# The low parts of the first phase's weights: ScalarE writes the rounded weights negated, and a DMA from GpSimd's queue adds the weights from DRAM

## The chip, the core and the metric

The kernel runs on one core of a Trainium2 chip. The metric is the time of one execution on the device, in microseconds (us). Three runs of the kernel before took 1390.13, 1390.4 and 1390.64 us; the median is 1390.4 us.

## The reference

Three layers run one after the other, all in float32.

```python
# 1. linear attention, 4 batches x 8 heads, 768 steps, head size 48
for t in range(768):
    state = alpha[t][:, None] * state + outer(k[t], v[t])
    y[t]  = q[t] @ state
x = y as (3072 tokens, 384)
# 2. four experts, 384 -> 1024 -> 384, all of them for every token
p = probs / (probs.sum(-1) + 1e-9)
x = sum over e of  p[:, e] * (relu(x @ w1[e]) @ w2[e])
# 3. one layer, 384 -> 2048 -> 384
h = x @ w_in;  out = (h * clip(h + 3, 0, 6) / 6) @ w_out
```

## The kernel before

Every large matmul is done in three passes of a faster number format. A float32 matrix A is split into a rounded part `hi` and the remainder `lo` = A - hi, and A @ B becomes hi@hi + lo@hi + hi@lo. For a weight slice `round_w` makes both parts: ScalarE copies the loaded slice into the rounding format (L770), VectorE subtracts (L772). The tiles are called w0h and w0l for a slice of w1, w1h and w1l for one of w2; the loaded slice is `rw`, or a room in a tile `early_h` or `early_l`. x is split in the same way into xh and xl (L789, L790), and the hidden layer into hh (ScalarE, from the matmul's result ph) and hl (VectorE, from ph and hh; L822, L825).

The experts' hidden units are cut into 16 slices of 256. The first phase goes with the first S0 = 7 slices over all tokens, while the attention of later tokens is still being computed; phases 1 and 2 take the other slices and the last layer. A step is half a slice (128 hidden units) for one block of tokens: `mm1` makes ph, then hh and hl; `mm2` of the step before adds into the accumulators po. The first block of 512 tokens is done in two halves of 256 tokens, which are one attention unit each, so the first pass over the 7 slices is 14 steps. In these steps the weights of the slices are still being split for the first time.

Attention runs in units of 256 tokens. One unit's work is a list of named pieces: products of q, k and alpha on VectorE, transposes and small matmuls on TensorE (pkt, pqt, pa, pk, pu, py), copies of their results on ScalarE (kt, qt, kc, qc, ktok, ys), and per unit one trip of the result to DRAM (x_d) and back (rx). `Attention.group` and `Attention.rest` put some pieces of the next unit behind each step.

TensorE, VectorE, ScalarE and SP carry out their instructions in the order in which the program writes them down (`manual_schedule`); a planner sets GpSimd's order. The list `todo` holds pairs of a step and a function: `next_w` splits one loaded slice at its step and, where that frees a room, issues the load of a later slice on SP's queue. Loads of slices 1 to 3 are issued before the steps begin. GpSimd clears tiles and cuts masks for the attention at the start, and decodes part of the last layer's weights much later; it issues no DMA.

Of the kernel before, what the change touches and what calls it, by code (L numbers as in the profile page):

```python
# [14 lines left out]
AF = mybir.ActivationFunctionType  # L15
# [3 lines left out]
P = 128  # L19
# [536 lines left out]
def tile_gla__then__moe__then__moe2(  # L556
# [29 lines left out]
    nc = tc.nc  # L586
# [4 lines left out]
    KT = DM // P  # L591
    NB = 512
    NBLK = N // NB
    SL = 2 * P
    S0 = 7
# [4 lines left out]
    mul, add, sub = ALU.mult, ALU.add, ALU.subtract  # L600
# [42 lines left out]
    w_out32 = dram.tile([F2, DM], F32, name="w_out32")  # L643
# [89 lines left out]
    wts, raws = {}, {}  # L733
# [6 lines left out]
    def rw(nm):  # L740
        nonlocal nraw
        if early:
            return early.pop(0)
        nraw += 1
        pool = rawq if late and nraw % 3 == 0 else rawp
        return pool.tile([P, 3 * SL], F32, tag="rw", name=nm)

    def load_w(y, i):
        e, c = slices[i]
        raw = rw(f"rw{y}_{i}")  # L750
        if y == 0:
            src = w_in32 if e is None else w1[e]
            nc.sync.dma_start(
                raw.rearrange("p (j f) -> p j f", j=KT), src[:, c : c + SL].rearrange("(j p) f -> p j f", p=P)
            )
        else:
            src = w_out32 if e is None else w2[e]
            nc.sync.dma_start(
                raw.rearrange("p (j m) -> p j m", j=2), src[c : c + SL, :].rearrange("(j p) m -> p j m", p=P)
            )  # L760
        raws[(y, i)] = raw

    def split_w(y, i):
        round_w(y, i)()

    def round_w(y, i):
        raw = raws.pop((y, i))
        pool = wpb if S0 <= i < S0 + SB or S1 <= i < S1 + SB else wpa
        hi, lo = (pool.tile([P, 3 * SL], F32R, tag=f"w{y}{z}", name=f"w{y}{z}_{i}") for z in "hl")
        nc.scalar.copy(hi, raw)  # L770
        wts[(y, i)] = [t.rearrange("p (j f) -> p j f", j=KT if y == 0 else 2) for t in (hi, lo)]
        return lambda: nc.vector.tensor_tensor(lo, raw, hi.bitcast(F32), op=sub)  # L772


# [159 lines left out]
            nc.sync.dma_start(out[r0 : r0 + P, :], o)  # L934


    ctx.enter_context(tc.manual_schedule(engines={mybir.EngineType.DVE, mybir.EngineType.Activation, mybir.EngineType.PE, mybir.EngineType.SP}))
    at_ctx = ExitStack()
    at = Attention(at_ctx, tc, q, k, v, alpha, x_d, psa, "psa", lambda n: load_x(0, n), lambda n: split_x(0, n))
    NU = at.NU  # L940
# [1 line left out]
    at.load_vd(0)  # L942
    at.load(0, "v")
    load_w(0, 0)
    nc.sync.dma_start(pr, probs.rearrange("(p i) e -> p i e", p=P))
    at.load_vt(0)
    load_w(1, 0)
    for z in "hl":
        e_ = xp.tile([P, KT * NB], F32, tag=f"x{z}", name=f"early_{z}")
# [3 lines left out]
    def again(x):  # L953

        early.append(rooms[x])
# [4 lines left out]
    def sw(y, i):  # L960
        split_w(y, i)
# [11 lines left out]
    busy(6)  # L973
    at.load(1, "qka")
    load_w(0, 1)
    load_w(1, 1)
    load_w(0, 2)
# [6 lines left out]
    busy(5)  # L984
    u("C3 y1 M2 K")
    lows = [round_w(0, 0), round_w(1, 0)]
    busy(5)
    u("y2 y3 y4 y5 U")
# [7 lines left out]
    at.load(1, "v")  # L996
    at.load_vd(1)
    low = round_w(0, 1)
    u("p2 r1 u0 u1 cp kq kk tp", 1)
    low()  # L1000
# [16 lines left out]
    todo = []  # L1017
# [28 lines left out]
    def next_w(y, i):  # L1046
        sw(y, i)
        if (y, i) in room_of and queue:
            room_of[queue[0]] = room_of[(y, i)]
            again(room_of[(y, i)])  # L1050
            load_w(*queue.pop(0))

    for y, i in order[order.index((1, 1)) :]:
        todo.append((2 * i - 2 + y, lambda y=y, i=i: next_w(y, i)))
    pend, rest = [], []
    period, at_step, begun = 0, 0, g
    last_b = (0, 0)
# [1 line left out]
    for vi, vv in enumerate(visits):  # L1059
# [16 lines left out]
        for f in range(len(vv["steps"])):  # L1076
# [29 lines left out]
            i, z = v2["steps"][done[1]]  # L1106
# [55 lines left out]
```

## Time and profile before

| | |
|---|---|
| median of three runs | 1390.4 us |
| the profiled execution | 1391.08 us, its span 1389.1 us |
| TensorE (PE) busy | 1360.7 us, 98% |
| VectorE (DVE) busy | 843.7 us, 61%, and 90% or more in many of the first slices |
| ScalarE (ACT) busy | 453.0 us, 33% |
| GpSimd (POOL) busy | 83.0 us, 6% |
| mean granted clock of TensorE | 0.993 of full speed |

Times in the rows are us from the start of the span. A row of the timeline has the start, the length, the engine, the line, the operation, what is written and read, and in square brackets how long the engine idled before and what ended that. A row of the stretches has the stretch, its length, then busy time and number of instructions of PE, PEld (weight loads), DVE, ACT and POOL, then TensorE's granted clock, the mean busy share of the 16 DMA engines, and GB/s. A row of the waits has the sum, the number of waits and the longest. SPq is SP's queue of DMA issues.

### The profile page before, as it was taken

How to read it: one execution, taken by the hardware profiler on the slowest of the kernel's cores; microseconds unless marked ns; L12 is line 12 of the kernel's file. 1: busy time of each engine (PE TensorE's matmuls, PEld its weight loads, DVE VectorE, ACT ScalarE, POOL GpSimd, SP SyncE). 2: the span in 40 equal slices, each digit the busy share in tenths (PEclk: the TensorE clock that was granted, in tenths of full speed). 3: DMA queues.
4: the chain of work that ended last, by engine and by line, in shares of the span. 5: the costliest groups of instructions: out<-in, count | busy, mean ns of one | idle time of the engine just before them, and what ended most of it. 6: DMA issues, size and time to landing. Idle time of an engine off the chain costs nothing.

```text
span 1389.1 us, 26360 instructions
## 1 busy us (share of the span) xinstructions
PE 1360.7 (98%) x11006; PEld 1137.7 (82%) x11006; DVE 843.7 (61%) x1524; ACT 453.0 (33%) x775; POOL 83.0 (6%) x125
## 2 busy tenths in 40 slices
PE   8788999999999999999999999999999999999998
PEld 7788887888878888888888888888888888888898
DVE  8998977767685268657566666645534343434332
ACT  3554444443434133111111111113333333333333
POOL 2000000000000001211111111100000000000000
PEclk9989999999999999999999999999999999999999
DMA  6654544344532256514242422324202020202010
GB/s 196 189 153 127 155 133 134 103 113 133 146 111 89 66 186 213 158 54 151 64 141 65 125 92 89 101 65 133 91 1 46 1 46 0 46 1 46 1 23 24
DMA packets 156551, 132.36 MB, mean 95 GB/s; under 512 B 65040, under 2 KB 138256, under 8 KB 156432
## 3 DMA queue, kind: packets, MB, share of 16 engines
q1 hardware_dynamic: 156432, 130.68, 32.5%
q8 instruction: 86, 1.41, 0.4%
q14 instruction: 33, 0.27, 0.1%
HBM read 100.71 MB, written 34.65 MB: 97 GB/s over the span
## 4 chain that ended last, share of the span: by engine, by line
PE 90%; DVE 5%; ACT 1%; DMA 1%; issue 1%; POOL 1%; SPq 0%; DVEq 0%; POOLq 0%
PE ph L814 41%; PE po L873 38%; PE po L875 2%; PE py L473 2%; PE py L494 1%; PE pa L374 1%; PE pu L419 1%; ACT qt L334 1%; DMA vl<-vd 1%; DVE qt L362 1%; DVE hl L825 1%; PE pk L400 1%; PE pkt L322 1%; PE py L457 1%; DVE kt L362 0%
## 5 line engine op out<-in xcount | busy, mean ns | idle before, releaser
L873 PE MATMUL po<-hl,w1h 128*128 128x512 f32 (+1 forms) x858 | 326.7, 381 | 7.5 <-DVE hl L825 7.5
L873 PE MATMUL po<-hh,w1h 128*128 128x512 f32 (+1 forms) x858 | 326.6, 381 | 4.8 <-ACT hh L822 2.9
L873 PE MATMUL po<-hh,w1l 128*128 128x512 f32 (+1 forms) x858 | 326.0, 380 | 0.0
L822 ACT ACTIVATE hh<-ph 128x512 fp32r<-128x512 f32 (+1 forms) x206 | 117.4, 570 | 510.6 <-PE ph L814 503.2
L825 DVE SCALAR_TENSOR_TENSOR hl<-ph,hh 128x512 fp32r<-128x512 f32 (+1 forms) x206 | 134.4, 652 | 241.5 <-ACT hh L822 241.5
L814 PE MATMUL ph<-xh,w0h 128*128 128x512 f32 (+1 forms) x906 | 256.3, 392 | 1.4 <-ACT xh L789 0.8
L814 PE MATMUL ph<-xh,w0l 128*128 128x512 f32 (+1 forms) x906 | 247.4, 382 | 0.0
L814 PE MATMUL ph<-xl,w0h 128*128 128x512 f32 (+1 forms) x906 | 246.8, 381 | 0.0
L873 PEld LDWEIGHTS po<-hl,w1h 128*128 128x128 f32 x858 | 162.6, 189 | 39.2 <-DVE hl L825 8.7
L814 PEld LDWEIGHTS ph<-xh,w0l 128*128 128x128 f32 x906 | 167.6, 190 | 33.0
L814 PEld LDWEIGHTS ph<-xl,w0h 128*128 128x128 f32 x906 | 167.5, 190 | 32.9 <-DVE xl L790 0.2
L873 PEld LDWEIGHTS po<-hh,w1h 128*128 128x128 f32 x858 | 162.5, 189 | 36.8 <-ACT hh L822 3.1
L814 PEld LDWEIGHTS ph<-xh,w0h 128*128 128x128 f32 x906 | 162.9, 189 | 34.8 <-DVE hl L825 1.4
L873 PEld LDWEIGHTS po<-hh,w1l 128*128 128x128 f32 x858 | 162.5, 189 | 30.0
L837 DVE SCALAR_TENSOR_TENSOR g<-g,ph 128x512 f32<-128x512 f32 (+1 forms) x97 | 66.2, 683 | 171.1 <-ACT g L833 171.1
L833 ACT ACTIVATE g<-ph,three 128x512 f32<-128x512 f32 (+1 forms) x97 | 66.2, 684 | 185.0 <-PE ph L814 185.0
L840 DVE SCALAR_TENSOR_TENSOR hl<-g,hh 128x512 fp32r<-128x512 f32 (+1 forms) x97 | 66.5, 686 | 66.6 <-ACT hh L838 66.6
L838 ACT ACTIVATE hh<-g 128x512 fp32r<-128x512 f32 (+1 forms) x97 | 60.9, 628 | 74.6 <-DVE g L837 74.6
L683 POOL TENSOR_TENSOR sq<-hc 128x256 f32<-128x256 f32 x48 | 34.4, 717 | 627.7 <-DMA pb<-p_d 496.4
L916 DVE TENSOR_TENSOR t<-po,pb 128x512 f32<-128x512 f32 (+1 forms) x82 | 52.6, 656 | 0.0
L698 POOL TENSOR_TENSOR a<-a,hc 128x256 f32<-128x256 f32 x48 | 38.7, 807 | 184.7 <-DVE hc L697 184.7
L352 ACT COPY kc<-kt 128x512 f32<-128x512 f32 x48 | 30.2, 630 | 58.1 <-PE pa L374 38.9
(106 smaller groups left out, 1191.5 us busy)
## 6 DMA issues: line engine op xcount, KB each, us to landing
rx<-x_d SPq DMA_DIRECT2D x36, 384.0 KB
vl<-vd SPq DMA_DIRECT2D x96, 96.0 KB
rw<-in_moe_w_dram SPq DMA_DIRECT2D x21, 384.0 KB
pb<-p_d SPq DMA_DIRECT2D x28, 256.0 KB
raw<-in_moe_w_in_dram SPq DMA_DIRECT2D x24, 256.0 KB
raw<-in_moe_w_out_dram SPq DMA_DIRECT2D x24, 256.0 KB
acc_d<-t SPq DMA_DIRECT2D x20, 256.0 KB
rq<-in_q_dram SPq DMA_DIRECT2D x24, 192.0 KB
```

What stands on the lines that cost most here:

```text
L352: nc.scalar.copy(c.rearrange("p x (b w) -> p (x b) w", w=self.W[l]), halves(z, l, x))
L683: nc.gpsimd.tensor_tensor(sq, hc, hc, op=mul)
L698: nc.gpsimd.tensor_tensor(a, a, hc, op=add)
L814: pe.matmul(ph[:, 0:n], w[:, j, fs], x[:, j, cs], start=(o == 0 and j == 0), stop=(o == 2 and j == KT - 1),)
L822: nc.scalar.activation(hh[:, 0:n], ph[:, 0:n], AF.Relu)
L825: nc.vector.scalar_tensor_tensor(hl[:, 0:n], ph[:, 0:n], 0.0, hh[:, 0:n].bitcast(F32), op0=ALU.max, op1=sub)
L833: nc.scalar.activation(g[:, c], ph[:, c], AF.Relu, bias=three)
L837: nc.vector.scalar_tensor_tensor(g[:, c], g[:, c], 6.0, ph[:, c], op0=ALU.min, op1=mul)
L838: nc.scalar.activation(hh[:, c], g[:, c], AF.Copy, scale=1.0 / 6.0)
L840: nc.vector.scalar_tensor_tensor(hl[:, c], g[:, c], 1.0 / 6.0, hh[:, c].bitcast(F32), op0=mul, op1=sub)
L873: pe.matmul(accs[vi][m][:, 0:n], w[:, z, ms], h[:, 0:n], **fl)
L916: nc.vector.tensor_tensor(t[:, 0:n], po[:, 0:n], pb, op=mul)
```

## The change

In the first phase's 7 slices the subtraction on VectorE goes. ScalarE reads the loaded slice a second time and writes it with the sign turned into the tile of the low part, rounded as the high part is; then a DMA of GpSimd's queue reads the slice again from DRAM and adds it into that tile, so that the tile holds slice - hi. The other slices are split as before. Every `next_w` runs one step earlier, and GpSimd's instructions, too, now stand in the program's order.

```diff
--- before.py
+++ after.py
@@ -745,19 +745,17 @@
         pool = rawq if late and nraw % 3 == 0 else rawp
         return pool.tile([P, 3 * SL], F32, tag="rw", name=nm)
 
-    def load_w(y, i):
+    def part(y, i):
         e, c = slices[i]
-        raw = rw(f"rw{y}_{i}")
         if y == 0:
             src = w_in32 if e is None else w1[e]
-            nc.sync.dma_start(
-                raw.rearrange("p (j f) -> p j f", j=KT), src[:, c : c + SL].rearrange("(j p) f -> p j f", p=P)
-            )
-        else:
-            src = w_out32 if e is None else w2[e]
-            nc.sync.dma_start(
-                raw.rearrange("p (j m) -> p j m", j=2), src[c : c + SL, :].rearrange("(j p) m -> p j m", p=P)
-            )
+            return src[:, c : c + SL].rearrange("(j p) f -> p j f", p=P)
+        src = w_out32 if e is None else w2[e]
+        return src[c : c + SL, :].rearrange("(j p) m -> p j m", p=P)
+
+    def load_w(y, i):
+        raw = rw(f"rw{y}_{i}")
+        nc.sync.dma_start(raw.rearrange("p (j f) -> p j f", j=KT if y == 0 else 2), part(y, i))
         raws[(y, i)] = raw
 
     def split_w(y, i):
@@ -769,6 +767,9 @@
         hi, lo = (pool.tile([P, 3 * SL], F32R, tag=f"w{y}{z}", name=f"w{y}{z}_{i}") for z in "hl")
         nc.scalar.copy(hi, raw)
         wts[(y, i)] = [t.rearrange("p (j f) -> p j f", j=KT if y == 0 else 2) for t in (hi, lo)]
+        if i < S0:
+            nc.scalar.activation(lo, raw, AF.Copy, scale=-1.0)
+            return lambda: nc.gpsimd.dma_start(wts[(y, i)][1], part(y, i), accum_op=add)
         return lambda: nc.vector.tensor_tensor(lo, raw, hi.bitcast(F32), op=sub)
 
 
@@ -934,7 +935,7 @@
             nc.sync.dma_start(out[r0 : r0 + P, :], o)
 
 
-    ctx.enter_context(tc.manual_schedule(engines={mybir.EngineType.DVE, mybir.EngineType.Activation, mybir.EngineType.PE, mybir.EngineType.SP}))
+    ctx.enter_context(tc.manual_schedule(engines={mybir.EngineType.DVE, mybir.EngineType.Activation, mybir.EngineType.PE, mybir.EngineType.SP, mybir.EngineType.Pool}))
     at_ctx = ExitStack()
     at = Attention(at_ctx, tc, q, k, v, alpha, x_d, psa, "psa", lambda n: load_x(0, n), lambda n: split_x(0, n))
     NU = at.NU
@@ -1051,7 +1052,7 @@
             load_w(*queue.pop(0))
 
     for y, i in order[order.index((1, 1)) :]:
-        todo.append((2 * i - 2 + y, lambda y=y, i=i: next_w(y, i)))
+        todo.append((2 * i - 3 + y, lambda y=y, i=i: next_w(y, i)))
     pend, rest = [], []
     period, at_step, begun = 0, 0, g
     last_b = (0, 0)
```

VectorE, around the steps 2 and 3 (hl_2, hl_3; kt and qt are the attention's running products, w0l and w1l low parts of slice 2), before:

```order
L362 TENSOR_TENSOR kt_755<-kt_755,tl_1_749 128x128x4
L362 TENSOR_TENSOR qt_824<-qt_824,tl_1_749 128x128x4
L772 TENSOR_TENSOR w0l_852<-early_l,w0h_851 128x768
L825 SCALAR_TENSOR_TENSOR hl_2_867<-ph_2_856,hh_2_866 128x256
L190 TENSOR_TENSOR w_2_870<-rq_708,rk_711 128x768
L247 TENSOR_REDUCE dg_2_872<-w_2_870 128x16
L362 TENSOR_TENSOR kt_755<-kt_755,tl_1_776 128x64x8
L362 TENSOR_TENSOR qt_824<-qt_824,tl_1_776 128x64x8
L772 TENSOR_TENSOR w1l_920<-early_l,w1h_919 128x768
L825 SCALAR_TENSOR_TENSOR hl_3_935<-ph_3_924,hh_3_934 128x256
```

and now:

```order
L362 TENSOR_TENSOR kt_764<-kt_764,tl_1_758 128x128x4
L362 TENSOR_TENSOR qt_834<-qt_834,tl_1_758 128x128x4
L826 SCALAR_TENSOR_TENSOR hl_2_878<-ph_2_867,hh_2_877 128x256
L190 TENSOR_TENSOR w_2_881<-rq_711,rk_714 128x768
L247 TENSOR_REDUCE dg_2_883<-w_2_881 128x16
L362 TENSOR_TENSOR kt_764<-kt_764,tl_1_785 128x64x8
L362 TENSOR_TENSOR qt_834<-qt_834,tl_1_785 128x64x8
L826 SCALAR_TENSOR_TENSOR hl_3_946<-ph_3_935,hh_3_945 128x256
```

Both subtractions are gone; nothing else changes its place.

ScalarE, around the steps 1 and 2 (hh_1, hh_2), before:

```order
L334 COPY kt_755<-pkt_1_757 128x8x16x4
L770 CAST w1h_784<-early_h 128x768
L822 ACTIVATE hh_1_799<-ph_1_789 128x256
L334 COPY qt_824<-pqt_1_825 128x8x16x4
L334 COPY qt_824<-pqt_1_826 128x8x16x4
L352 COPY kc_1_845<-kt_755 128x512
L352 COPY qc_1_847<-qt_824 128x512
L770 CAST w0h_851<-early_l 128x768
L822 ACTIVATE hh_2_866<-ph_2_856 128x256
```

and now:

```order
L334 COPY kt_764<-pkt_1_766 128x8x16x4
L768 CAST w0h_793<-early_l 128x768
L771 ACTIVATE w0l_794<-early_l 128x768
L823 ACTIVATE hh_1_809<-ph_1_799 128x256
L334 COPY qt_834<-pqt_1_835 128x8x16x4
L334 COPY qt_834<-pqt_1_836 128x8x16x4
L352 COPY kc_1_855<-kt_764 128x512
L352 COPY qc_1_857<-qt_834 128x512
L768 CAST w1h_861<-early_l 128x768
L771 ACTIVATE w1l_862<-early_l 128x768
L823 ACTIVATE hh_2_877<-ph_2_867 128x256
```

In front of each hh stands one weight pass more, and the slice that is split there is the one that had its turn one step later.

GpSimd at the start (ident, mask, vl and sc are tiles of the attention), before:

```order
masks.py:197 MEMSET ident 128x128
L85 MEMSET mask 128x256
L101 MEMSET vl 128x1600
L105 MEMSET sc_144 128x208
masks.py:199 ISA
masks.py:199 AFFINE_SELECT ident<-ident 128x128
L105 MEMSET sc_145 128x208
L105 MEMSET sc_146 128x208
L105 MEMSET sc_147 128x208
L90 AFFINE_SELECT mask<-mask 64x64 x8
```

and now, from the last mask selections on:

```order
L90 AFFINE_SELECT mask<-mask 64x64
L94 AFFINE_SELECT mask<-mask 64x64
L101 MEMSET vl 128x1600
L105 MEMSET sc_144 128x208
L105 MEMSET sc_145 128x208
L105 MEMSET sc_146 128x208
L105 MEMSET sc_147 128x208
L105 MEMSET sc_148 128x208
L772 DMA w0l_457<-in_moe_w_dram 128x3x256
L772 DMA w1l_461<-in_moe_w_dram 128x2x384
L772 DMA w0l_687<-in_moe_w_dram 128x3x256
```

All 16 mask selections (L90, L94) now come before vl and sc are cleared, and the first adding loads follow.

## Rows read from the trace of the kernel before

**Rows 1.** Stretches of the span on all engines (columns as told above).

```profile
43.30:66.50 23.20, 16.71 (x222) 14.59 (x222) 22.55 (x43) 13.80 (x24) 0.00 (x0) 0.99 0.73 213
66.50:72.70 6.20, 6.16 (x65) 5.70 (x66) 6.16 (x14) 3.54 (x9) 0.00 (x0) 0.50 0.46 147
72.70:84.00 11.30, 11.30 (x294) 10.52 (x294) 8.27 (x21) 5.10 (x11) 0.00 (x0) 0.99 0.69 177
84.00:96.70 12.70, 9.76 (x130) 9.11 (x126) 12.42 (x22) 7.47 (x13) 0.00 (x0) 0.73 0.45 121
96.70:112.50 15.80, 13.29 (x315) 12.02 (x314) 15.39 (x32) 6.80 (x15) 0.00 (x0) 1.00 0.42 131
157.30:1389.00 1231.70, 1227.67 (x8572) 1015.95 (x8572) 702.92 (x1245) 376.31 (x625) 73.14 (x96) 1.00 0.30 87
```

**Rows 2.** Waits of TensorE from 30 to 165 us, the longest in total.

```profile
PE po L873 <- DVE hl L825: 7.5, 6, 2.4
```

**Rows 3.** Timeline from 54 to 67 us: low parts, and TensorE's waits for hl.

```profile
55.30 0.95 DVE L772 TENSOR_TENSOR w0l<-early_l,w0h 128x768 fp32r<-128x768 f32 x1
...
56.64 0.39 PE L873 MATMUL po<-hl,w1h 128*128 128x256 f32 x1 [1.89 <-DVE hl L825]
...
60.89 0.39 PE L873 MATMUL po<-hl,w1h 128*128 128x256 f32 x1 [1.02 <-DVE hl L825]
...
65.20 0.95 DVE L772 TENSOR_TENSOR w0l<-rw,w0h 128x768 fp32r<-128x768 f32 x1
...
66.07 0.42 DVE L825 SCALAR_TENSOR_TENSOR hl<-ph,hh 128x256 fp32r<-128x256 f32 x1
...
66.54 0.58 PE L873 MATMUL po<-hl,w1h 128*128 128x256 f32 x1 [2.42 <-DVE hl L825]
```

**Rows 4.** Timeline from 36 to 43 us: slice 1's rounding and the first block of x.

```profile
36.11 0.83 ACT L770 CAST w0h<-early_h 128x768 fp32r<-128x768 f32 x1
...
39.02 0.38 SPq L780 DMA_DIRECT2D rx<-x_d  x1
...
42.43 0.83 ACT L789 CAST xh<-rx 128x768 fp32r<-128x768 f32 x1 [1.49 <-DMA rx<-x_d]
```

**Rows 5.** Timeline from 69 to 75 us: the way to the state update.

```profile
69.27 0.55 DVE L203 TENSOR_TENSOR rk<-rk,ra 128x384 f32<-128x384 f32 x1
...
70.87 1.06 ACT L408 COPY ktok<-pk 128x512 f32<-128x512 f32 x2
...
73.84 1.15 PE L419 MATMUL pu<-vt,ktok 64*64 64x48 f32 x64
```

**Rows 6.** Timeline from 83.5 to 94 us: the pass over the second half block.

```profile
83.92 0.96 DVE L772 TENSOR_TENSOR w0l<-early_l,w0h 128x768 fp32r<-128x768 f32 x1 [2.51 <-ACT w0h L770]
...
89.06 0.83 ACT L770 CAST w1h<-early_h 128x768 fp32r<-128x768 f32 x1
89.38 0.75 DVE L916 TENSOR_TENSOR t<-po,pb 128x256 f32<-128x256 f32 x2
89.80 0.37 ACT L822 ACTIVATE hh<-ph 128x256 fp32r<-128x256 f32 x1
...
90.27 0.55 PE L873 MATMUL po<-hh,w1h 128*128 128x256 f32 x1 [2.94 <-ACT hh L822]
...
93.67 0.62 ACT L352 COPY kc<-kt 128x512 f32<-128x512 f32 x1 [2.53 <-PE pa L374]
```

**Rows 7.** DMA queue of SP from 36 to 112 us: packets, MB, share of 16 engines.

```profile
q1 hardware_dynamic: 15032, 12.37, 56.7%
```

**Rows 8.** Timeline of the first 13 us: GpSimd's work and the first load into vl.

```profile
1.19 1.44 POOL L101 MEMSET vl<- 128x1600 f32 x1
...
3.76 2.59 POOL L90 TENSOR_SCALAR_AFFINE_SELECT mask<-mask 64x64 f32<-64x64 f32 x8
...
6.74 4.57 POOL L94 TENSOR_SCALAR_AFFINE_SELECT mask<-mask 64x64 f32<-64x64 f32 x8
...
11.06 1.91 SPq L151 DMA_DIRECT2D vl<-vd  x3
```

## The prediction

> **What bounds the kernel now.** I read the slices of the page first, then the span cut into stretches, then who TensorE waited for, then the timeline around those waits. The stretches [rows 1] show two kernels in one. From 157.3 us to the end TensorE is busy for 1227.67 of 1231.70 us: what another engine does there can shorten the run by 4 us at most. Before it, the attention units and the first weight slices share the engines, and VectorE is the full one: 22.55 of 23.20 us from 43.3, 6.16 of 6.20, 12.42 of 12.70, 15.39 of 15.80, with one looser stretch from 72.7 (8.27 of 11.30), in which TensorE never stands still. TensorE's granted clock is 0.50 (1.2 GHz) from 66.5 to 72.7 and 0.73 in the mean from 84. From 30 to 165 us TensorE waited longest for VectorE's low halves `hl`: 7.5 us in 6 waits [rows 2]. What the change gains must come out of these 114 us; behind them the kernel only slides.
>
> **What it removes.** 14 subtractions of 128x768 on VectorE (L772), 0.95 us each, 0.87 from its start to the start of the next instruction (65.20 to 66.07) [rows 3]. 14 x 0.87 = 12.2 us of VectorE's time, but not all of it on the path.
>
> Up to 43.3 us, three of them (slice 0's two and slice 1's w0l). The first hidden-layer matmul waits for the first block of x, which goes out to DRAM and comes back: its load is issued at 39.02, and ScalarE, after 1.49 us of idling, rounds it at 42.43 [rows 4]. VectorE is ready earlier and then waits for that block too: 0.
>
> 43.3 to 66.5. Slice 1's w1l comes first, but the `hl` behind it also needs ScalarE's `hh`, which has one 128x768 pass more in front of it: 0. Then three subtractions stand in front of three `hl` for which TensorE idles 1.89, 1.02 and 2.42 us [rows 3]; two of the three are shown there, the third, before 60.89, lies in the same place. Each takes 0.87 off the chain: the first wait becomes 1.0, the second 0.15, the third 1.6. **Term 1: -2.6 us.**
>
> 66.5 to 72.7. VectorE loses two more subtractions here, but TensorE is what runs, at 1.2 GHz, right after the longest of those waits. At 2.4 GHz the 6.2 us would be 3.1. The three waits in front shrink from 5.3 to 2.8 us in sum, and a wait of 1.89 at 56.64 was not followed by a lower clock (0.99 over 43.3 to 66.5), so I take it that the clock stays up. Not all of 3.1 comes back, since the state update `pu`, at 73.84, needs `ktok`, the last of five copies on ScalarE behind VectorE's rk product [rows 5]. The product follows the next `hl`, and that follows an `hh` behind ScalarE's two weight passes: `hl` at about 66.0, product done at 67.0, then 1.05 to the start of `ktok` (69.82 to 70.87 now) and 1.06 for it: 69.1. From 73.84 that is 4.7, of which 2.6 are term 1. **Term 2: -2.1 us**, its ends 0 and -3.1.
>
> 72.7 to 84. TensorE alone; the two subtractions there: 0.
>
> 84 to 112.5. The w0l at 83.92 waited 2.51 us for ScalarE's w0h [rows 6]. It goes, and in its place stands ScalarE's second pass in front of `hh`: 0.73 (w1h at 89.06 to hh at 89.80) for 0.87, so -0.1. The next subtraction goes as well, but the kt and qt products two instructions later then wait for ScalarE's kc at 93.67, which waits for TensorE's pa: a good half is given back, -0.4. The last is worth what `hh` lets through, about -0.5. TensorE's 2.94 us before 90.27 are put down to `hh`, but they end together with VectorE's two t products, 89.38 + 0.75 = 90.13, which free the accumulators: that wait moves along with VectorE's chain and keeps its length. **Term 3: -1.0 us**, its ends 0 and -2.6.
>
> **What it adds on ScalarE.** 14 passes of 128x768 at 0.73: 10.2 us on an engine that is busy 13.80 of 23.20 and 7.47 of 12.70 us [rows 1]. Those up to 43.3 lie in idle time. The others lie in front of a step's `hh`, and terms 1 to 3 have them in. Weights are split one step earlier than before, so step 0 gets one too, where ScalarE waits for the first `ph` anyway: 0.
>
> **What it adds on GpSimd and the DMA engines.** 14 adding loads of 384 KB. GpSimd is idle from 11.3 us until the second layer's weights are decoded. Each load is issued behind ScalarE's negated copy, and TensorE reads the result three steps later, a step being 4 to 6 us by the three waits of [rows 3]. No adding load runs before, so its cost is bounded. From 36 to 112 us SP's queue, which carries nearly all, took 56.7% of 16 engines for 12.37 MB [rows 7]: 43 us, 3.5 us a MB, some 1.35 us for a plain 384 KB. An adding load also reads its destination: 1.35 if that is free, 2.0 for three movements instead of two, 4.05 for three whole loads. I take 2.0 to 2.7, nearest to the plain load. The twelve in that stretch are 24 to 32 us; 33 us were free. They fit, just: 0.
>
> One collision is on the path. Slice 1's two copies on ScalarE end at about 36.11 + 2 x 0.83 = 37.8, so its adding load moves while the first block of x is fetched, 39.02 to 42.43 [rows 4]. Where x gives way to one plain load's share it is 1.35 late; the ends are 0 (the adding comes after it) and 2.7 (two shares). **Term 4: +1.35 us.**
>
> SP's loads of later slices wait for ScalarE's passes and no longer for VectorE; one moves ahead of unit 1's vt and vl, 0.4 us of issue, and vl is not read before `pu`: 0. On GpSimd the 16 mask selections now come before the memset of vl. Before, vl is cleared at 2.63 and the selections end at 11.31, while SP's first load into vl goes out at 11.06 [rows 8]. Turned round, vl is cleared some 1 us before 11.3 (five small memsets lie behind it). If it were 2 us late, vl would still land long before its reader, in the 30s: 0.
>
> **Sum.** -2.6 - 2.1 - 1.0 + 1.35 = -4.35. The profiled execution took 1391.08 (span 1389.1): 1386.7. The median of the runs is 1390.4, 0.68 below it, so I predict 1386.0. A measurement of this kernel tells a change from none from about 0.2%, 2.8 us.
>
> **A rule against this change.** VectorE's subtractions have two inputs and take 0.95 us for 768 columns each time [rows 3, 6]. The Trainium skill, SBUF — State Buffer, section "Who interferes with whom", says that GpSimd cannot write a DMA's descriptors while VectorE runs in a two-port mode, which copies, casts and tensor_scalar can enter and tensor_tensor cannot; its summary advises against hiding such a DMA under VectorE. By its letter it costs nothing here; by its advice it is the rival "starved".
>
> **Rivals.**
> *The clock falls as before*, since the third wait is still 1.6 us. Then term 2 is 0 and the time 1390.4 - 2.25 = 1388.1, with the collision at its end 1389.5. For: the clock also fell somewhere in the stretch from 84, with its wait of 2.94. Against: 1.6 is shorter than either wait beside a fall. Within 0.2%. Chance 0.25.
>
> *The DMA engines are full* (slower). From 33/12 = 2.75 us of all 16 engines per adding load they run behind, and vl, q, k and the next slices come late. At 4.05, 48.6 - 33 = 15.6 more than was free: 1386.0 + 15.6 = 1401.6; at 3.4 each, 1394. For: their share is 0.73 already from 43.3 to 66.5 [rows 1]. Against: every load here has a deadline of several us. The Trainium skill, DMA: Bandwidth & Descriptors, section "Issuing engines are not separate DMA queues", says that DMAs share the same 16 engines whoever issues them; before, one queue carries nearly all, so no row shows it. Chance 0.18, most of it near 1394.
>
> *Starved*: GpSimd can write descriptors only in VectorE's gaps. From 43.3 to 72.7 there are 0.7 us of them [rows 1]; slice 2's w0l, due between the waits at 56.64 and 60.89, would come in the gap before 83.92: +25, 1415. Against: beside VectorE's first products GpSimd's mask selections slow down, 4.57 us for eight where eight took 2.59, and go on [rows 8]. Chance 0.05.
>
> *All of it*: ScalarE keeps up, and the eleven subtractions from 43.3 on all shorten the chain, 9.6 us: 1390.4 - 9.6 + 1.35 = 1382. Against: rows 6. Chance 0.06.
>
> **Numbers.** My forecast has 0.46, and its own range is 1383 (terms 2 and 3 at their far ends) to 1387.5. With "all of it" faster has 0.52; same 0.25; slower 0.23. The range for 8 in 10 leaves out most of "all of it", "starved" and the worse half of the full DMA engines: 1382.5 to 1396.
>
> **What would show it.** Right: the waits at 56.64, 60.89 and 66.54 become about 1.0, 0.15 and 1.6; the clock behind them stays at 1.0; TensorE's first matmul on x is about 1.35 later than now and, counted from there, `pu` comes 4.7 earlier; more of the waits end with ScalarE. Wrong: a wait of TensorE for w0l or w1l that ends with a DMA; x over 3 us late; a clock of 0.5 after the third wait; adding loads that land over 10 us after ScalarE's copy.

## The result: slower by 0.7%

| | before | changed |
|---|---|---|
| median of the runs | 1390.52 us (1390.13 to 1390.93) | 1399.76 us (1398.48 to 1402.1) |
| ratio, with its 95% interval | | 1.0067 [1.0054, 1.008] |
| span of the profiled execution | 1389.1 us | 1398.0 us |

The forecast was 1386.0, in a range up to 1396. What happened is the second rival, the DMA engines running full, in the stretch where the loads fall.

The stretches of [rows 1], now of the changed kernel:

```profile
43.30:66.50 23.20, 17.53 (x221) 15.57 (x221) 17.22 (x35) 17.65 (x28) 5.78 (x5) 0.93 1.01 242
66.50:72.70 6.20, 4.12 (x67) 3.45 (x67) 5.74 (x14) 4.25 (x10) 1.65 (x2) 1.00 1.15 271
72.70:84.00 11.30, 5.47 (x157) 4.78 (x156) 6.83 (x17) 3.96 (x7) 2.48 (x2) 0.89 1.07 225
84.00:96.70 12.70, 12.46 (x207) 11.56 (x206) 3.41 (x9) 5.85 (x12) 1.20 (x1) 0.83 0.75 194
96.70:112.50 15.80, 12.71 (x162) 11.76 (x160) 14.24 (x27) 10.62 (x20) 2.48 (x2) 0.78 0.81 158
```

VectorE is freer (17.22 of 23.20 us where it was 22.55), and the clock from 66.5 to 72.7 is 1.00 where it was 0.50. But the DMA share, last but one number, is 1.01, 1.15 and 1.07 where it was 0.73, 0.46 and 0.69. A share above 1 says that the times of packets overlap on an engine; no stretch shown here goes above 1.2, and I take 1 as full. TensorE's busy time from 72.7 to 84 falls from 11.30 to 5.47 us.

The timeline of the changed kernel, with the rows that answer to [rows 3 to 6]: TensorE's waits, the first block of x, `ktok`, and the adding load of slice 1's w0l on GpSimd.

```profile
38.77 1.28 POOL L772 DMA_DIRECT2D w0l<-in_moe_w_dram  x1 [7.05 <-ACT kp L209]
...
39.83 0.38 SPq L781 DMA_DIRECT2D rx<-x_d  x1
...
45.77 0.83 ACT L790 CAST xh<-rx 128x768 fp32r<-128x768 f32 x1 [6.31 <-DMA rx<-x_d]
...
46.66 0.62 PE L815 MATMUL ph<-xh,w0h 128*128 128x256 f32 x3 [3.40 <-ACT xh L790]
...
60.23 0.39 PE L874 MATMUL po<-hl,w1h 128*128 128x256 f32 x1 [1.01 <-DVE hl L826]
...
63.62 0.39 PE L874 MATMUL po<-hl,w1h 128*128 128x256 f32 x1 [0.16 <-DVE hl L826]
...
68.40 0.39 PE L874 MATMUL po<-hl,w1h 128*128 128x256 f32 x1 [1.48 <-DVE hl L826]
...
71.90 0.62 PE L815 MATMUL ph<-xh,w0l 128*128 128x256 f32 x3 [0.59 <-DMA w0l<-in_moe_w_dram]
...
72.39 1.06 ACT L408 COPY ktok<-pk 128x512 f32<-128x512 f32 x2
...
75.76 1.15 PE L419 MATMUL pu<-vt,ktok 64*64 64x48 f32 x64 [1.81 <-DMA vt<-vd]
...
80.92 0.69 PE L473 MATMUL py<-asb,vl 64*64 64x64 f32 x32 [3.11 <-DMA vl<-vd]
...
82.53 1.12 PE L473 MATMUL py<-asb,vl 64*64 64x64 f32 x28 [0.91 <-DMA vl<-vd]
...
100.04 0.55 PE L874 MATMUL po<-hh,w1h 128*128 128x256 f32 x1 [3.09 <-DVE t L917]
```

The three waits for `hl` are now 1.01, 0.16 and 1.48 us, as forecast (1.0, 0.15, 1.6). The loss stands elsewhere: x is rounded 5.94 us after its load was issued (39.83 to 45.77) where that took 3.41 [rows 4], and TensorE waits for DMAs that it did not wait for in this part of the span before: w0l (0.59), vt (1.81) and vl (3.11 and 0.91). `ktok` began at 72.39, so `pu` could have started near 73.5; vt held it to 75.76.

The DMA queues from 36 to 112 us, as in [rows 7]:

```profile
q1 hardware_dynamic: 13485, 10.64, 50.7%
q0 software_dynamic: 3972, 4.64, 38.9%
```

The adding loads are queue 0. A load is 4704/14 = 336 packets, so 3972 packets are 11.8 loads, and 38.9% of 76 us is 29.6: 2.50 us of 16 engines for each. The chain of waits of the changed kernel, from 40 to 120 us, goes through three transfers of SP's queue (start, length):

```profile
39.83 5.92 DMA rx<-x_d
...
63.09 12.54 DMA vt<-vd
...
75.69 13.57 DMA vl<-vd
```

In the chain of the kernel before vt is absent, vl holds 4.24 us and rx 3.39. The lengths run from issue to landing. SP itself was held up as well: its eight issues for unit 1's vl took 12.40 us (63.80 to 76.20) where they took 6.24 before, and the 13.57 are those of the last of the eight.

**Where the time goes.** Three points bound the account: TensorE's first matmul on x, the matmul `ptt` that stood at 112.53 us before (121.04 now), and the end. The stretch between the first two, before, changed, and changed without the adding loads (first experiment):

```profile
43.32:112.53 69.21, 57.22 (x1016) 51.94 (x1016) 64.80 (x129) 36.70 (x70) 0.00 (x0) 0.90 0.58 166
```

```profile
46.66:121.04 74.38, 59.48 (x1015) 53.32 (x1015) 55.61 (x118) 43.81 (x80) 13.60 (x11) 0.89 0.88 205
```

```profile
43.68:108.92 65.24, 54.53 (x1016) 49.36 (x1016) 55.53 (x118) 44.48 (x81) 0.00 (x0) 0.95 0.61 177
```

Against the last of them the changed kernel loses 46.66 - 43.68 = 3.0 us up to x, 74.38 - 65.24 = 9.1 between, and 1.7 behind (1276.96 against 1275.28): 13.8, the difference of the spans. Of the 9.1, TensorE is 59.48 - 54.53 = 5.0 us longer busy at the same matmuls, at a lower clock (0.89 against 0.95), and 4.2 longer idle. The clock fell behind waits for DMAs:

```profile
46.60:49.00 2.40, 2.33 (x11) 1.80 (x11) 2.33 (x4) 1.79 (x4) 0.61 (x1) 0.68 1.15 230
49.00:51.00 2.00, 2.00 (x21) 1.87 (x21) 1.90 (x7) 1.53 (x4) 0.58 (x1) 0.53 1.01 323
...
82.00:84.00 2.00, 1.47 (x30) 1.36 (x31) 0.00 (x0) 0.00 (x0) 0.00 (x0) 0.50 1.18 254
84.00:86.00 2.00, 2.00 (x11) 2.00 (x11) 0.00 (x0) 0.04 (x1) 0.00 (x0) 0.50 0.99 294
86.00:88.00 2.00, 2.00 (x11) 1.81 (x9) 0.42 (x1) 0.34 (x1) 0.00 (x0) 0.50 1.01 296
```

It is 0.68 and 0.53 behind the 3.40 us for x, and 0.50 (1.2 GHz) from 82 to 88, behind the waits for vl.

### The profile page after: what moved, and what is told of

Same layout as the page of the kernel before. It is cut to its first block, busy times and chain, and to the rows that moved or that the text cites. A ratio compares the mean times of both kernels' runs of the same rounds, so it can differ in the third digit from the quotient of the medians.

```text
span 1398.0 us, 26375 instructions
## 1 busy us (share of the span) xinstructions
PE 1363.6 (98%) x11006; PEld 1139.6 (82%) x11006; DVE 832.1 (60%) x1510; ACT 463.0 (33%) x789; POOL 99.4 (7%) x139
## 3 DMA queue, kind: packets, MB, share of 16 engines
q0 software_dynamic: 4704, 5.51, 2.5%
## 4 chain that ended last, share of the span: by engine, by line
PE 89%; DMA 5%; DVE 2%; ACT 2%; issue 1%; POOL 1%; SPq 0%; DVEq 0%; POOLq 0%
PE ph L815 41%; PE po L874 38%; PE po L876 2%; DMA vl<-vd 2%; PE pa L374 1%; PE py L473 1%; PE py L494 1%; DMA rx<-x_d 1%; DMA vt<-vd 1%; ACT qt L334 1%; PE pu L419 1%; PE pkt L322 1%; PE pqt L322 0%; PE pk L400 0%; PE py L457 0%
```

## The experiments

The kernel before took 1390.55 us beside the first four, 1390.93 beside the next four and 1390.41 beside the last four. Ratios are to it.

**The adding loads taken out.**

```diff
-            return lambda: nc.gpsimd.dma_start(wts[(y, i)][1], part(y, i), accum_op=add)
+            return lambda: None
```

> The changed kernel with ScalarE's negated copies but without the 14 adding loads (the low parts stay -hi, so the result is not the reference's). Theory D, the adding loads take the DMA engines from SP's loads of x, vt and vl: without them the first matmul on x is back near 43.3 us, TensorE's waits for vt and vl (6 us from 75 to 84) are gone, and the time is what was forecast without the collision, 1390.5 - 5.7 = 1385, at most 1388. Rival A, ScalarE's second pass in front of every hh, and the earlier splitting, make the loss: 1396 to 1400 as with the adding loads. Rival P, GpSimd's order at the start: the 0.8 us by which x's load is issued later stays (39.8 instead of 39.0).

1386.28 us, 0.9969 [0.9959, 0.9979]. The load of x and its rounding, TensorE's waits, and `pu`:

```profile
39.55 0.38 SPq L781 DMA_DIRECT2D rx<-x_d  x1
...
42.80 0.83 ACT L790 CAST xh<-rx 128x768 fp32r<-128x768 f32 x1 [3.52 <-DMA rx<-x_d]
...
43.68 0.62 PE L815 MATMUL ph<-xh,w0h 128*128 128x256 f32 x3 [0.62 <-ACT xh L790]
...
56.26 0.39 PE L874 MATMUL po<-hl,w1h 128*128 128x256 f32 x1 [1.04 <-DVE hl L826]
...
59.65 0.39 PE L874 MATMUL po<-hl,w1h 128*128 128x256 f32 x1 [0.16 <-DVE hl L826]
...
64.43 0.39 PE L874 MATMUL po<-hl,w1h 128*128 128x256 f32 x1 [1.55 <-DVE hl L826]
...
69.07 1.60 PE L419 MATMUL pu<-vt,ktok 64*64 64x48 f32 x64
...
76.38 0.41 PE L309 MATMUL ptt<-ident,tp 128*128 128x128 f32 x2 [1.63 <-DVE sc L448]
...
87.92 0.55 PE L874 MATMUL po<-hh,w1h 128*128 128x256 f32 x1 [3.08 <-DVE t L917]
```

So everything but the loads gains 4.3 of the 5.7 us that terms 1 to 3 promised (1384.7), and the loads cost 13.5 us: they are the whole loss.

**Plain loads on the same queue.** GpSimd's DMA overwrites the tile.

```diff
-nc.gpsimd.dma_start(wts[(y, i)][1], part(y, i), accum_op=add)
+nc.gpsimd.dma_start(wts[(y, i)][1], part(y, i))
```

> The changed kernel whose 14 DMAs on GpSimd's queue overwrite the low parts instead of adding to them (the low parts hold the whole weights, so the result is not the reference's). Same descriptors and bytes from DRAM, no reading of the destination. The adding loads took 31.8% of 16 engines over 110 us, 2.5 us each, against 1.35 for a plain load of SP. Theory D with the price in the adding: about 1.35 each, 1387 to 1390. Theory D with the price in a second queue's bytes as such: 2.5 each again and 1397 to 1400. Rival A: 1397 to 1400.

1389.55 us, 0.9994 [0.9984, 1.0003]. Queue 0 of this kernel, and of the changed one, from 20 to 130 us (14 loads in each):

```profile
q0 software_dynamic: 4704, 5.51, 22.2%
```

```profile
q0 software_dynamic: 4704, 5.51, 31.8%
```

22.2% of 110 us by 14 is 1.74 us for a plain load (1.35 expected), 31.8% is 2.50 for an adding one. The same packets and bytes without the adding cost 3.3 us, with it 13.5: a second queue and GpSimd's issuing are at most a quarter of the loss. The mean DMA share doesn't tell the two kernels apart: over 40.7 us from about the first matmul on x it is 1.04 in the changed kernel and 1.02 with plain loads, against 0.71 without any. What tells them apart is what was left to SP's queue. Its packets, MB and share in that stretch: changed kernel (46.7 to 87.4), plain loads (44.6 to 85.3), no loads (43.7 to 84.4):

```profile
q1 hardware_dynamic: 6841, 6.65, 55.4%
```

```profile
q1 hardware_dynamic: 8438, 7.75, 65.7%
```

```profile
q1 hardware_dynamic: 10419, 8.21, 70.0%
```

**Only the earlier splits**, in the kernel before.

```diff
-        todo.append((2 * i - 2 + y, lambda y=y, i=i: next_w(y, i)))
+        todo.append((2 * i - 3 + y, lambda y=y, i=i: next_w(y, i)))
```

> The kernel before with one edit: every split of a weight slice one step earlier, VectorE subtracting as before. It moves the same load ahead of vt and vl on SP's queue as the change does. Theory D: SP's order costs little, 1389 to 1392. Rival S, the load that now goes ahead of vt and vl delays them: 1393 or more, with TensorE waiting for vl.

1389.64 us, 0.9995 [0.9986, 1.0004]: the new order of the splits and of SP's loads costs nothing by itself.

**Adding from slice 2 on**, and **adding in slices 0 and 1 alone**; the other slices subtract on VectorE.

```diff
-        if i < S0:
+        if 2 <= i < S0:
```
```diff
-        if i < S0:
+        if i < 2:
```

> The changed kernel in which slices 0 and 1 are subtracted by VectorE as before; adding loads only from slice 2 on (10 instead of 14). Theory D: the first block of x is fetched without an adding load beside it, its first matmul comes 2.5 us earlier than in the changed kernel (44.1 instead of 46.7); the waits for vt and vl stay, about 1396 to 1397.5. If the collision at the start was the whole loss: 1390 or less. Rival A: no change, 1399.

> The changed kernel with adding loads in slices 0 and 1 only (4 of 14). Theory D: the first matmul on x is 2.5 to 3.4 us late as in the changed kernel, and nothing else changes: 1390.5 + 3 = 1393 to 1394.5. If x is not held up by the adding load: 1390 to 1391.

From slice 2 on: 1395.56 us, 1.0034 [1.0021, 1.0047], a little under the 1396 to 1397.5 expected. x is in time (first matmul at 42.89), and TensorE waits 2.45 and 1.75 us for vl; the wait for vt is gone, and 2.51 us for w1l stand in its place. Slices 0 and 1 alone: 1394.15 us, 1.0022 [1.0012, 1.0033]. Here x is late, and nothing else:

```profile
38.16 1.28 POOL L772 DMA_DIRECT2D w0l<-in_moe_w_dram  x1 [6.35 <-ACT kp L209]
...
39.89 0.38 SPq L781 DMA_DIRECT2D rx<-x_d  x1
...
45.75 0.83 ACT L790 CAST xh<-rx 128x768 fp32r<-128x768 f32 x1 [6.89 <-DMA rx<-x_d]
...
46.64 0.58 PE L815 MATMUL ph<-xh,w0h 128*128 128x256 f32 x1 [3.99 <-ACT xh L790]
```

Beside one adding load, issued 1.73 us before x's, x's load takes 5.86 us to its rounding where it took 3.41 [rows 4]. The first matmul moves from 43.32 to 46.64; the other 0.87 us are x's load going out later, and no run ties them to the adding load. Otherwise the later waits are those of the kernel before (1.86 and 2.27 for `hl`, 2.94 for `hh`). The two halves are 5.0 and 3.2 us slower than the kernel before them, the whole change 9.2: each half loses by itself.

**Two passes on ScalarE, subtraction kept** (the kernel before; VectorE overwrites the negated tile).

```diff
         wts[(y, i)] = [...]
+        if i < S0:
+            nc.scalar.activation(lo, raw, AF.Copy, scale=-1.0)
         return lambda: nc.vector.tensor_tensor(lo, raw, hi.bitcast(F32), op=sub)
```

> The kernel before in which ScalarE writes the negated weights into the low parts too, and VectorE then overwrites them by its subtraction: ScalarE's 14 second passes alone, at their old steps. VectorE's subtraction waits for one pass more, and hh comes 0.73 us later in each of 11 steps. By the steps of the prediction nearly all of it lies beside VectorE's full chain: 1390.5 to 1393. If the passes were the price of the change (rival A): 1396 or more.

1394.03 us (runs from 1390.89 to 1394.5), 1.0013 [1.0004, 1.0022]: above the 1390.5 to 1393 expected, below the rival's 1396. With the subtraction still behind the passes, TensorE's longest wait for `hl` is 2.48 us and the one for `hh` 3.68 (2.42 and 2.94 before). The passes don't explain the loss: the first experiment has them too, and is faster than the kernel before.

**GpSimd subtracts.** No second pass, no DMA.

```diff
-            nc.scalar.activation(lo, raw, AF.Copy, scale=-1.0)
-            return lambda: nc.gpsimd.dma_start(wts[(y, i)][1], part(y, i), accum_op=add)
+            return lambda: nc.gpsimd.tensor_tensor(lo, raw, hi.bitcast(F32), op=sub)
```

> The kernel before with splits one step earlier, GpSimd in the program's order, and the first 7 slices' low parts subtracted by GpSimd: no second pass on ScalarE, no adding load. GpSimd's two-input product of 256 columns took 0.72 to 0.81 us, so about 2.3 us for 768 columns, 14 of them in 75 us, each with three steps until TensorE reads it. If VectorE and GpSimd run side by side: a little better than without any adding load, 1384 to 1387. If they take turns at SBUF, VectorE's products beside a subtraction grow by up to 2.3 us each, up to 32 us in all of which a third to a half lies on the path: 1395 to 1403.

1399.54 us, 1.0062 [1.0049, 1.0074]: as slow, by another way; TensorE waits for no DMA from 36 to 130 us. Groups of VectorE's instructions from 43 to 113 us (behind the first bar their busy time in us and the mean of one in ns), first of the kernel before:

```profile
L362 DVE TENSOR_TENSOR kt<-kt,tl 128x512 f32<-128x512 f32 x8 | 5.5, 684 | 0.0
...
L238 DVE TENSOR_TENSOR w<-rq,rk 128x384 f32<-128x384 f32 x6 | 3.1, 551 | 0.0
```

```profile
L362 DVE TENSOR_TENSOR kt<-kt,tl 128x512 f32<-128x512 f32 x8 | 8.9, 1107 | 0.0
...
L238 DVE TENSOR_TENSOR w<-rq,rk 128x384 f32<-128x384 f32 x4 | 5.3, 1368 | 0.0
```

In the mean these two-input products grow from 684 to 1107 and from 551 to 1368 ns. One by one, the three kt products that run beside one of GpSimd's subtractions (1.8 to 2.2 us each) take 1.73, 1.96 and 1.75 us, and the other five 0.68 or 0.69. The Trainium skill, SBUF — State Buffer, section "Who interferes with whom", says that a VectorE instruction with two SBUF inputs contends with a GpSimd instruction that reads SBUF; these rows agree.

**Adding in slices 2, 5 and 6 alone.**

```diff
-        if i < S0:
+        if i in (2, 5, 6):
```

> The changed kernel with adding loads in slices 2, 5 and 6 only (6 of 14); slices 0, 1, 3, 4 are subtracted by VectorE. The loads that go are the two that moved beside x and the four that were issued from 62 to 75 us, beside vt and vl. Theory D: no long wait for x, vt or vl; two of the three subtractions of term 1 saved: 1388 to 1391. Rival A2, the extra bytes as such slow whatever runs then, 9.2 us x 6/14: 1394.5.

1391.04 us, 1.0001 [0.9992, 1.001]. No wait for x, vt or vl, but one of 1.90 us for w1l: in sum nothing is gained or lost.

**SP's slice loads behind vt and vl.** Then what is late? Two slice loads of 384 KB move behind unit 1's vt and vl.

```diff
-            again(room_of[(y, i)])
-            load_w(*queue.pop(0))
+            room, nxt = room_of[(y, i)], queue.pop(0)
+            def fetch():
+                again(room)
+                load_w(*nxt)
+            if i < 3:
+                after(2, fetch)
+            else:
+                fetch()
```

> The changed kernel, with two slice loads (384 KB each) on SP's queue moved from before unit 1's vt and vl to behind them; nothing is left out. Theory (DMA engines full, and the loads nearest to the path pay): vt and vl go out about 4 us earlier and meet two loads less, so TensorE's waits for vt (1.8) and vl (3.1 and 0.9) shrink to 0 to 2 in sum and the fall of the clock behind them goes: 1392 to 1396 us, while the two moved loads land later and rounding may wait for them. Rival (the adding loads themselves hold the engines, whatever stands in SP's queue): the waits stay within 1.5 us and the time at 1398 to 1401. Rival (slice loads are as urgent): a new wait of TensorE for hh or w0l, 1399 to 1404.

1402.87 us, 1.0091 [1.0077, 1.0105]. The theory's 1392 to 1396 fails, and the last rival, that slice loads are as urgent, holds: the waits for vt and vl shrink to 0.57 us, and this stands in their place in the timeline:

```profile
67.34 1.97 SPq L758 DMA_DIRECT2D early_l<-in_moe_w_dram  x1
...
81.02 0.83 ACT L768 CAST w1h<-early_l 128x768 fp32r<-128x768 f32 x1 [9.69 <-DMA early_l<-in_moe_w_dram]
...
82.92 0.58 PE L874 MATMUL po<-hh,w1h 128*128 128x256 f32 x1 [6.23 <-ACT hh L823]
```

ScalarE idles 9.69 us for the slice, and TensorE 6.23 behind it. In both orders the load that goes last takes long: vt 12.5 and vl 13.6 us in the changed kernel, the slice 13.7 here by the chain of waits. But full engines are not all of it. The slice landed at 81.0, and just before that the DMA share was low:

```profile
79.00:81.00 2.00, 0.00 (x0) 0.00 (x0) 0.00 (x0) 0.00 (x0) 0.00 (x0) 0.73 0.15 55
```

A share of 0.15 is as much as two or three of the 16 engines at work, so most of their time went unused while the end of the slice was still on its way. Why it came so slowly no run here shows.

**The same, with adding from slice 2 on** (the diff above and `2 <= i < S0` together).

> Both remedies: slices 0 and 1 subtract on VectorE as before, slices 2 to 6 are added by the DMA, and the two slice loads go behind unit 1's vt and vl. Nothing is left out. Theory: x in time (xh at about 42.0), the waits for vl small, TensorE's wait for slice 2's w1l (2.5) stays: 1388 to 1392 us. Rival (lateness only moves to the next load): 1394 to 1397, as with slices 2 to 6 alone (1395.6).

1400.2 us, 1.007 [1.0057, 1.0082]. x in time (first matmul at 43.81), again 6.1 us for `hh`, with a DMA share of 0.21 from 76 to 79 us, the end of the late slice's load: the theory's 1388 to 1392 fails, the rival holds in kind, and even its 1394 to 1397 was too low.

**Adding from SBUF.** The source is the slice that ScalarE read.

```diff
-nc.gpsimd.dma_start(wts[(y, i)][1], part(y, i), accum_op=add)
+nc.gpsimd.dma_start(lo, raw, accum_op=add)
```

> The changed kernel, with the adding load's source changed from DRAM to the slice that already lies in SBUF; the rooms come free only after the adding. Nothing is left out. Theory (the price is the adding into SBUF, not the bytes from DRAM): queue 0 takes the same 2.2 to 2.8 us of 16 engines a load, x stays about 3 us late, 1397 to 1404 us. Rival (reading DRAM beside SP's loads is what costs): queue 0's share falls to half or less, and the time to 1388 to 1393.

1396.77 us (runs from 1395.06 to 1401.6, the profiled one the slowest), 1.0042 [1.0029, 1.0056]: just under the theory's 1397 to 1404, far from the rival's 1388 to 1393. x is rounded 5.17 us after its load was issued. From 20 to 130 us:

```profile
q0 software_dynamic: 2016, 5.51, 28.5%
```

28.5% of 110 us by 14 is 2.24 us a load, without a byte read from DRAM. Four kernels now differ in the price of a load (in the third, SP's later loads also wait until the adding has read the slice):

| loads on queue 0 | us of 16 engines each | median, us |
|---|---|---|
| none | 0 | 1386.28 |
| plain, from DRAM | 1.74 | 1389.55 |
| adding, from SBUF | 2.24 | 1396.77 |
| adding, from DRAM | 2.50 | 1399.76 |

The first 1.74 cost 3.3 us, the next 0.76 another 10.2. That fits a resource that runs full between the two; no run varies the price by itself.

**GpSimd's order left to the planner.**

```diff
-..., mybir.EngineType.SP, mybir.EngineType.Pool}))
+..., mybir.EngineType.SP}))
```

> The changed kernel, but GpSimd's order is left to the planner, as in the kernel before. Theory (the loss is the adding loads): the same within 1.5 us, 1398 to 1401. Rival (the mask selections that now come before the memset of vl delay unit 0): the issue of rx comes 0.8 us earlier, at 39.0, and the time falls by about as much, to 1397 to 1399.

1398.09 us, 1.0058 [1.0046, 1.0071], within the range of both readings. rx was issued at 40.09, not earlier, and three kernels that keep GpSimd's order as in the change issued it at 38.52 to 38.79 (adding from slice 2 on, adding in slices 2, 5 and 6, slice loads behind vt and vl). So the mask selections have no part in the loss.

No kernel that computes the whole was faster than before by more than the measurement can tell.

## Why the prediction was wrong

- **The step that failed is "They fit, just: 0".** The price in it was right: 2.50 us a load, within "2.0 to 2.7", though at the far end from the plain load. The room was wrong. "33 us were free" is the mean over 76 us, and the loads don't spread over these. From 43.3 to 84 [rows 1] shows what was taken: 0.73 x 23.2 + 0.46 x 6.2 + 0.69 x 11.3 = 27.6 us, so 13.1 were free. Eight adding loads went out in that stretch of the steps, which is 3.4 us later in the changed kernel (46.7 to 87.4; GpSimd's groups there, below): 8 x 2.50 = 20.0 us, by this estimate 6.9 more than there was. The share of SP's queue there shows it: 55.4% of 40.7 us where it had 70.0% without the loads, 5.9 us less. The plain loads, 8 x 1.74 = 13.9, just about fit, and their kernel lost little. The loss from the first matmul on x to `ptt` is 9.1 us, of which 5.0 are TensorE busy for longer at a lower clock.

```profile
L772 POOL DMA_DIRECT2D w0l<-in_moe_w_dram x4 | 5.1, 1280 | 10.9 <-ACT hh L823 10.4 <-ACT w0l L771 0.5
L772 POOL DMA_DIRECT2D w1l<-in_moe_w_dram x4 | 4.8, 1198 | 17.4 <-ACT hh L823 9.1 <-ACT w1l L771 8.3
```

- **The rival "the DMA engines are full"** was the cause, and its own threshold, 2.75 us a load, was the same mean: by the stretch it is 13.1 / 8 = 1.6, an estimate too. Its objection, "every load here has a deadline of several us", was wrong in size: vt and vl took 12.5 and 13.6 us. The prediction checked that vl "is not read before `pu`" and didn't ask how long it would take in a full queue.
- **Term 4** (+1.35, ends 0 and 2.7) was the right place and came out at its far end: x's load took 5.94 us to its rounding against 3.25 without the adding loads (39.55 to 42.80), 2.7 longer, two plain loads' share. The load also went out 0.28 later, so the first matmul came 3.0 later (46.66 against 43.68), and a lower clock followed the wait (0.68, then 0.53).
- **Term 1** (-2.6) held: the waits are 1.04, 0.16 and 1.55 without the loads, and the third ends 20.75 us after the first matmul on x where it ended 23.22 after it, 2.5 less.
- **Term 2** (-2.1) held: the clock from 66.5 to 72.7 is 1.00, with the adding loads and without, and `pu` comes 69.07 - 43.68 = 25.39 us after that matmul, where it came 30.52 after it: 5.1 earlier, 4.7 forecast. The rival "the clock falls as before" falls.
- **Term 3** (-1.0) was not there: from `pu` to `ptt` the kernel without loads took 39.85 us against 38.69, since VectorE's state update made TensorE wait 1.6 us at 76.38, in a stretch put down as 0. Behind `ptt`, where no term was, it was 1.3 faster, which makes up for it. That the wait of 2.94 us before 90.27 keeps its length was right (3.08), and it is now put down to VectorE's t.
- **"Starved"** falls: GpSimd's adding loads took 1.19 to 1.28 us each on its own engine beside a busy VectorE, and one began 0.3 us after ScalarE's negated copy (70.14 to 70.45). **"All of it"** needed 1382; without the loads it was 1386.3.
- Of the four signs named for "wrong" three came: TensorE waited for w0l (0.59 us, ended by a DMA), x came 3.3 us late against the kernel before (46.66, 43.32), and two adding loads, issued at 65.67 and 76.96, landed 10.2 and 10.5 us later. The clock behind the third wait stayed up.
- The order of SP's loads (0) and of GpSimd's start (0) were right.

## What to carry to other kernels

Before giving a DMA work that an engine did, take the DMA share of the stretch in which the loads fall, not of the whole phase: free time there, divided by the number of loads there, is the price that a load may have. Then look at what the old queue still moves there: the mean share alone hid the difference here. In the two orders tried another order of the loads only chose which one was late; and a late load cost more than its wait here, since TensorE's granted clock was lower behind the waits.

## What the runs showed of the hardware

- An adding DMA of 384 KB in float32 into SBUF took 2.50 us of the 16 engines in packet time (from DRAM) or 2.24 us (from SBUF, in fewer packets), a plain one from DRAM, with the packets of the first, 1.74 us. In the changed kernel it landed 6.8 us (w0l) or 7.8 us (w1l) after its issue in the median, at most 10.5, the plain one in its kernel after 4.3 or 5.3. The price did not hang on the number of loads in these two kernels: with four of them (slices 0 and 1 alone) queue 0 took 9.1% of 110 us, again 2.50 each.
- Beside one adding load of GpSimd's queue, issued 1.73 us before a load of SP's queue, that load took 5.86 us to its reader; in the eight kernels with no load of GpSimd's queue beside it, 3.21 to 3.42, and beside a plain one 4.15. The Trainium skill, DMA: Bandwidth & Descriptors, section "Issuing engines are not separate DMA queues", says that all issuers share the 16 engines; the runs agree (SP's queue at 55.4% where it had 70.0%).
